# Reordered queues of the vector, scalar, GpSimd and DMA engines beside a fixed TensorE sequence

## The chip, the cores and the metric

The kernel runs on one core of one Trainium2 chip. The core has five engines with a queue of instructions each: TensorE (PE, with its weight loads PEld), VectorE (DVE), ScalarE (ACT), GpSimd (POOL) and SyncE (SP), which here issues DMAs. Each engine works through its own queue in order, and steps on different engines are tied together by semaphores. The metric is the time of one execution in microseconds; of several executions the median counts.

## The reference

The reference is a recurrent attention (RWKV-7) followed by a normalised SwiGLU feed-forward, all in float32. There are 4 x 8 heads, 768 steps of time, and head size 40. The state S of each head is a 40 x 40 matrix:

```
y[t]  = r[t] @ S
Sa    = S @ a[t]
S     = S * w[t] - outer(Sa, b[t]) + outer(v[t], k[t])
```

The outputs of all heads make up x with 3072 rows and 320 columns, and then

```
xn  = x / sqrt(mean(x*x) + 1e-6) * rms_g
g   = xn @ w_gate
out = (silu(g) * (xn @ w_val)) @ w_out        # w_gate, w_val: 320 x 1536
```

## The kernel before

The 768 steps of time are cut into 24 chunks of 32. The work falls into four kinds of stages, each of which puts its steps into a list (`Plan.add`, line 280):

- **front(c)** (line 652) loads r-independent inputs of chunk c on POOL's queue, turns them with TensorE, and builds products of decays by levels of 1, 2, 4, 8 and 16. It fills the triangular matrices LT by masked copies on VectorE (`where`, COPY_PREDICATED), among them three near the diagonal. After that LT goes to DRAM as sB in four quarters, and comes back in another layout as M in four parts, all on SP's queue.
- **inverse(c)** (line 760) solves a triangular system on VectorE: 31 pairs of `tmp` and `Yi` steps, each dependent on the one before. The result goes out as sY in parts and returns into LT in four quarters (LT<-sY). `early_inverse` (line 778) does this for the first four chunks in another way.
- **main(c)** (line 810) does the recurrence for chunk c: matmuls with the state and with LT, the copies of their results into VU, the new state ST, the scores As, and the output y by levels. It ends with the norm (x) and the scaled, turned xg. Two chunks make a group.
- **feed(g)** (line 939) does the feed-forward for a group of two chunks: 12 slices of weights, loaded again for each group into five buffers wf (wf<-sW, 480 KB each, on SP's queue). Each slice has matmuls into PSUM, a Silu on ScalarE (sg), a product on VectorE (hT), and matmuls into the accumulator po. `narrow` (line 973) makes the weights into float32 once, in the first third.

The order is written out by hand. `Plan.issue` (line 322) takes two long strings of numbers. ORDER has 6179 words. A word n stands for the n-th step from the first one that has not been issued yet, and "-" for a pair of filler matmuls that keep TensorE active. As the program is built in this order, each engine's queue is that order, cut down to its own steps. Moving a word so that it passes only words of other engines changes no queue.

PAIRS has one digit for each of 499 *rooms*. A room is the PSUM space of one result of TensorE, and the digit says which of three pairs of banks (the tiles ps) it gets. A room has its pair from the first matmul that writes it to the last step that reads it; the next room on the same pair has to wait for that. So a step of VectorE or ScalarE that reads a room is waited for twice: by those who use its result, and by TensorE when it wants the pair.

In the profile nearly all steps have the line of a helper: VectorE L444, ScalarE L464 (activation), L467 (copy) and L470 (scale), POOL L473, DMA issues L483, matmuls L486, and transposes on TensorE L489. Steps are told apart by their tiles and times.

The lines around which the masked copies and the inverse turn are these:

```
where(LT...[:, :, :, dist:], near[:, dist - 1:dist]..., g4[:, :, :, at:at + m])     # front, three times
tt(tmp, Y[:, 0:n, i:i + 1]..., M[:, i:i + 1, i + 1:]..., MUL)                       # inverse, 31 times
tt(Y[:, 0:n, i + 1:], Y[:, 0:n, i + 1:], tmp, SUB)
```

Of the kernel before, what the change touches and what calls it, by code (L numbers as in the profile page):

```python
# [102 lines left out]
0 181 565 549 548 544 599 344 566 345 15 564 551 237 0 345 346 551 395 560 347 544 561 397 348 0 236 558 3 544 348 545  # L103
237 554 573 349 561 350 586 351 397 570 572 352 0 553 396 565 394 551 4 567 397 552 438 395 570 349 581 350 571 572
562 351 5 352 353 354 355 398 563 578 579 0 563 398 665 399 355 356 0 356 572 357 4 399 524 0 357 522 358 7 359 573
577 512 360 574 513 8 572 361 581 362 363 582 364 365 580 401 366 9 583 10 411 405 406 0 409 405 403 0 403 425 392 393
0 390 575 396 572 355 408 356 574 357 358 407 359 573 718 360 361 400 434 362 717 363 435 364 398 365 707 368 0 402
705 366 403 365 708 404 718 408 405 707 0 0 713 576 0 576 577 578 406 383 407 441 0 407 571 408 383 2 409 0 577 571
409 578 2 579 718 580 0 47 218 219 220 293 48 221 356 49 222 0 222 357 610 223 356 369 775 49 620 279 361 776 374 50
619 362 293 51 280 609 52 373 66 372 282 360 385 383 55 224 628 225 226 56 295 627 227 618 386 2 418 228 384 294 3 617  # L110
71 1 382 398 229 395 394 0 0 172 348 173 174 349 175 300 176 0 13 176 177 1 178 300 179 180 181 182 309 183 304 308 2
311 3 0 180 317 308 301 318 220 316 13 181 315 0 298 217 299 219 178 308 218 19 220 179 6 229 326 180 309 330 325 181
324 0 229 181 182 183 328 184 309 322 185 220 186 0 186 187 231 188 0 270 188 189 317 271 190 234 280 237 0 215 277
329 330 331 315 224 328 13 314 0 414 222 226 339 225 20 229 0 230 339 183 227 321 184 185 223 186 232 322 233 187 331
188 189 330 190 4 191 234 192 332 323 235 333 193 231 195 5 194 6 241 236 0 236 542 237 544 241 336 535 335 239 545
334 0 332 0 236 530 193 408 531 240 532 241 409 242 541 7 243 411 244 245 548 246 338 339 0 336 243 190 337 547 735
338 546 193 339 545 4 244 191 608 744 551 13 245 552 745 192 246 563 0 729 545 0 542 556 747 17 553 567 241 737 558 2
543 242 736 570 566 746 552 582 568 551 569 547 579 578 591 555 590 334 3 554 8 335 563 565 564 0 561 8 335 336 547
337 548 0 335 336 546 6 337 555 338 339 14 340 0 340 6 397 341 571 342 343 0 548 391 337 562 393 338 563 0 548 393 434
564 391 558 568 338 435 339 567 340 341 394 342 560 343 573 0 574 343 573 394 661 395 0 343 557 344 0 567 394 518 344  # L120
345 509 346 347 397 508 569 348 349 573 519 3 350 400 351 398 8 401 568 352 578 353 354 576 355 0 352 573 5 353 354
575 395 398 402 438 355 400 404 6 356 357 403 401 358 0 358 576 404 398 359 577 405 360 578 406 361 575 407 652 408 0
361 362 410 363 364 411 409 365 0 718 365 407 366 369 710 388 368 411 707 367 412 709 651 413 389 719 414 653 415 717
580 416 581 720 582 725 583 417 584 708 585 586 663 587 726 981 588 370 418 589 727 0 586 415 736 1142 728 986 416 741
0 752 975 416 728 431 723 659 586 738 986 417 1142 572 441 418 751 749 739 421 587 573 748 588 366 589 761 750 426 0
589 367 725 783 0 589 982 590 367 762 591 658 981 365 420 592 991 2 593 659 992 771 758 722 594 0 594 424 595 420 596
429 597 722 598 599 0 0 8 3 309 308 311 178 179 224 180 9 181 182 10 304 225 183 184 227 185 0 182 183 317 301 343 184
0 178 179 6 295 0 300 295 15 310 179 216 304 16 308 214 307 225 326 305 321 180 322 181 0 319 225 181 182 324 333 305
# [5 lines left out]
398 546 542 13 547 401 231 550 3 574 232 543 560 233 544 0 230 231 541 581 545 554 555 550 438 553 330 331 332 232 333  # L134
552 0 333 564 570 571 567 232 566 565 550 579 561 0 0 332 395 333 576 560 575 0 333 573 560 395 396 435 662 570 397
521 334 335 512 336 337 400 572 338 522 339 340 511 341 0 570 404 579 402 581 405 400 578 5 580 401 0 405 0 339 408
405 340 406 341 342 407 401 582 343 344 583 4 345 409 581 346 347 580 348 410 349 411 415 350 351 5 352 353 416 6 412
0 347 708 348 349 350 710 0 350 351 716 434 352 353 405 708 354 406 435 355 409 706 356 0 356 717 357 409 358 718 410
359 411 716 360 648 361 412 0 361 412 362 0 412 362 576 721 365 577 413 578 363 579 580 647 364 581 722 987 582 583 0
583 975 735 648 584 722 585 976 413 723 383 727 414 586 441 0 727 984 657 738 383 2 739 586 737 3 414 571 587 751 1140  # L140
588 415 763 748 589 772 750 1 590 416 660 572 364 749 0 226 293 358 394 227 52 776 228 66 294 359 229 360 55 368 367
617 60 230 628 231 382 370 395 627 232 233 618 234 67 235 3 236 61 237 418 0 61 237 0 237 54 238 0 184 11 12 185 186
306 187 188 0 188 0 188 0 185 317 186 301 343 8 187 188 13 189 302 303 220 190 191 308 9 192 315 312 221 193 316 223
194 0 217 307 215 311 306 226 323 321 16 322 326 3 317 320 227 188 189 190 218 191 332 333 334 0 315 188 266 189 215
323 277 0 187 10 264 188 189 328 221 273 190 191 20 414 339 222 192 311 193 322 195 340 194 223 196 323 332 324 0 230
330 333 226 241 225 332 223 4 545 229 227 536 228 224 535 231 546 5 196 6 232 534 533 335 0 234 336 542 235 335 543
233 333 236 232 0 0 235 194 612 0 235 193 232 13 191 233 192 404 236 237 3 334 238 239 4 335 336 337 338 240 550 544
339 752 5 340 0 0 735 539 334 335 538 728 0 539 736 551 543 540 737 556 16 568 745 580 0 14 588 543 540 725 554 553
734 548 564 544 565 0 562 548 0 564 0 546 571 540 556 547 0 540 556 438 541 553 550 328 569 329 554 390 565 552 330 0
330 580 331 391 332 567 333 334 335 336 225 337 550 0 391 565 0 224 336 563 0 336 390 337 224 392 338 225 339 0 390  # L150
225 434 339 226 392 567 340 566 227 341 575 393 0 0 555 392 393 556 571 570 557 0 337 505 569 338 391 339 564 506 340
341 439 656 516 515 342 394 343 566 223 344 0 564 344 574 394 0 574 400 571 395 572 394 344 398 403 345 399 0 345 346
401 347 348 396 2 404 395 576 403 349 577 350 351 575 352 409 353 574 354 3 355 0 399 409 404 355 0 0 713 352 353 401
714 573 354 402 705 432 355 406 403 356 703 574 357 358 359 384 716 360 361 407 706 362 408 363 0 714 384 408 363 409
703 645 364 575 410 0 440 575 576 410 577 3 578 645 579 0 410 579 580 1 581 656 582 646 411 0 220 49 221 222 355 50
777 295 51 296 52 357 610 223 0 52 293 620 775 360 55 355 617 357 358 369 361 627 374 223 60 610 224 362 359 619 373
382 618 368 367 363 628 61 370 371 372 66 2 364 383 0 379 384 385 0 53 362 415 378 0 327 338 309 341 168 350 169 170
337 318 171 5 349 321 0 171 9 172 338 319 173 0 317 173 174 0 171 172 5 316 329 328 330 324 334 173 13 6 174 175 220
176 325 341 327 0 214 332 216 335 0 318 214 15 332 169 328 170 216 16 171 172 173 217 174 330 175 0 175 176 328 217
336 337 419 226 339 0 337 176 223 0 225 176 177 3 178 179 223 267 180 181 266 182 183 226 184 277 185 186 276 236 228  # L160
339 227 8 338 238 234 341 340 230 229 4 233 187 231 239 232 188 245 189 190 9 191 5 192 237 193 194 539 345 195 235
196 346 537 6 197 244 198 240 540 0 234 192 541 235 540 239 236 340 531 16 341 3 342 408 542 240 543 241 335 343 242
344 243 0 332 240 341 241 342 343 544 13 344 242 345 189 346 0 344 345 544 731 346 542 240 347 402 241 348 543 349 556
20 742 242 350 561 0 731 403 572 350 242 351 740 546 544 584 352 739 547 0 187 547 747 544 186 557 748 558 185 568 567
570 737 188 603 352 242 552 548 0 552 0 351 578 553 0 553 562 351 563 560 546 0 15 351 546 352 547 560 5 565 0 574 0
585 237 554 586 351 4 570 572 571 555 575 556 569 352 576 353 566 354 5 355 6 356 397 357 582 567 358 0 561 352 574
391 353 0 392 353 354 434 575 393 570 355 391 435 356 357 576 394 571 0 357 579 571 394 580 358 581 359 360 578 361
395 362 0 362 363 4 364 395 365 510 366 0 508 366 4 367 368 518 369 370 371 659 519 372 407 373 376 5 6 397 409 582 8
399 583 400 581 403 398 375 374 405 406 9 580 404 408 401 402 410 416 10 411 415 724 412 657 377 413 715 417 414 717 0
718 411 709 412 580 651 719 581 413 435 414 707 372 388 653 415 720 374 582 583 373 416 584 585 577 371 586 417 587  # L170
389 0 414 584 415 585 586 587 416 659 588 589 432 417 590 574 721 591 1143 592 593 1142 594 418 0 721 985 418 722 976
735 421 726 441 0 739 992 722 726 3 658 751 982 1 763 727 2 783 738 431 983 593 0 351 316 572 0 238 326 328 563 172
# [875 lines left out]
```

## Time and profile before

| what | value |
|---|---|
| three timed runs | 1074.34, 1081.09, 1081.99 us (median 1081.09) |
| the profiled execution | 1082.16 us, span of its instructions 1080.3 us |
| TensorE | 1023.1 us busy, 95% of the span |
| VectorE | 850.2 us, 79% |
| ScalarE | 470.6 us, 44% |
| POOL | 309.5 us, 29% |
| mean granted TensorE clock | 0.967 |

Busy time is the time in which an engine had an instruction at work. The page also follows back the chain of work that ended last, and says for each idle time what ended it. A row of a timeline has the start, the length, the engine, the line, the operation, what is written and read (out<-in), the shape and the count; in square brackets stand the idle time of the engine just ahead of it and what ended that. Rows with SPq are DMA issues in SP's queue: their length is that of the issue and not of the transfer. A row of stretches has the length, then busy time and count by engine, the granted clock, the DMA engines' share and GB/s.

### The profile page before, as it was taken

The page shows a single profiled execution, that of the slowest core. Times are in us where ns is not written, and L with a number is a line of the kernel's source. Part 1 is how long each engine was busy: PE and PEld are TensorE (multiplying, and loading weights), DVE is VectorE, ACT ScalarE, POOL GpSimd, SP SyncE. Part 2 cuts the span into 40 slices and gives each one's busy share as a digit, 9 for nine tenths or more (in the row PEclk, how much of TensorE's full clock was granted, in tenths as well). Part 3 has the DMA queues.
Part 4 walks back from the last instruction along what each step waited for, and adds up shares of the span by engine and source line. Part 5 has one row for each costly group of instructions (what it writes and reads, how often), then busy time and mean ns, then how long its engine had stood idle before and what let it go on. Part 6 is the DMA issues. An engine that isn't in the chain of part 4 may idle for free.

```text
span 1080.3 us, 53530 instructions
## 1 busy us (share of the span) xinstructions
PE 1023.1 (95%) x23406; PEld 840.3 (78%) x23406; DVE 850.2 (79%) x2861; ACT 470.6 (44%) x1043; POOL 309.5 (29%) x554
## 2 busy tenths in 40 slices
PE   6878899999999999999999999999999999999998
PEld 6767777877888777787778778778777887887876
DVE  7877768966868988888898789979879889797321
ACT  6846755743443434433434334434425334432211
POOL 9714504130532141341332231331322321210000
PEclk9677989999999999999999999999979999999999
DMA  9965428775564483664465555564636555444252
GB/s 179 206 149 121 73 67 217 227 151 158 126 153 122 105 170 90 152 124 129 123 148 119 129 144 113 126 137 131 153 71 145 123 129 144 121 116 113 79 151 75
DMA packets 172458, 143.35 MB, mean 133 GB/s; under 512 B 125504, under 2 KB 143872, under 8 KB 172224
## 3 DMA queue, kind: packets, MB, share of 16 engines
q1 hardware_dynamic: 153856, 116.96, 42.4%
q0 software_dynamic: 16192, 22.64, 11.9%
q8 instruction: 184, 3.01, 1.2%
q10 hardware_dynamic: 2176, 0.33, 0.3%
q14 instruction: 50, 0.41, 0.1%
HBM read 123.86 MB, written 15.99 MB: 129 GB/s over the span
## 4 chain that ended last, share of the span: by engine, by line
PE 73%; DVE 13%; DMA 5%; ACT 4%; issue 3%; SPq 1%; POOL 0%; ACTq 0%; DVEq 0%
PE ps L486 50%; PE po L486 12%; PE ps L489 9%; DVE LT L444 2%; DVE tmp L444 2%; DVE y L444 2%; DVE Yi L444 2%; SPq L483 1%; DVE K L444 1%; PE po L1015 1%; DMA LT<-sY 1%; DVE As L444 1%; DMA rn<-in_r_dram 1%; DMA wf<-in_moe_w_gate_dram 1%; DVE hT L444 1%
## 5 line engine op out<-in xcount | busy, mean ns | idle before, releaser
L486 PE MATMUL ps<-xg,wf 128*128 128x256 f32 (+1 forms) x1728 | 358.6, 395 | 4.2 <-DVE xg L444 1.9
L486 PEld LDWEIGHTS ps<-xg,wf 128*128 128x128 f32 (+1 forms) x1728 | 263.9, 191 | 61.6 <-issue 15.9
L486 PE MATMUL po<-wf,hT 128*128 128x320 f32 x576 | 179.9, 445 | 1.8 <-issue 1.3
L464 ACT ACTIVATE sg<-ps 128x256 f32<-128x256 f32 x144 | 53.5, 383 | 239.0 <-PE ps L486 236.4
L444 DVE TENSOR_TENSOR tmp<-Yi,M 128x60 f32<-128x60 f32 (+24 forms) x620 | 130.1, 210 | 17.1 <-DMA M<-sB 2.7
L444 DVE TENSOR_TENSOR Yi<-Yi,tmp 128x60 f32<-128x60 f32 (+24 forms) x620 | 129.8, 209 | 13.9
L483 POOL DMA_DIRECT2D VU<-in_v_dram x92 | 53.2, 584 | 285.9 <-PE ps L486 149.0
L486 PEld LDWEIGHTS po<-wf,hT 128*128 128x128 f32 x576 | 102.0, 189 | 37.3 <-issue 3.7
L444 DVE TENSOR_TENSOR hT<-ps,sg 128x256 f32<-128x256 f32 x144 | 59.5, 420 | 67.5 <-ACT sg L464 66.2
L444 DVE TENSOR_TENSOR K<-K,T 128x512 f32<-128x512 f32 (+1 forms) x192 | 93.9, 499 | 11.7 <-PE ps L486 5.4
L486 PEld LDWEIGHTS ps<-Ab,K 40*64 40x64 f32 x4608 | 78.9, 139 | 30.0 <-issue 10.5
L486 PE MATMUL ps<-Ab,K 40*64 40x56 f32 x4608 | 89.1, 226 | 11.2 <-issue 2.4
L467 ACT COPY K<-K 128x256 f32<-128x256 f32 (+1 forms) x168 | 71.3, 442 | 60.5 <-PE ps L486 42.8
L444 DVE TENSOR_TENSOR As<-ps,msi 128x256 f32<-128x256 f32 (+1 forms) x186 | 78.4, 475 | 15.8 <-PE ps L486 15.0
L467 ACT COPY KN<-ps 128x640 f32<-128x640 f32 x96 | 66.1, 690 | 54.2 <-PE ps L489 22.1
L483 POOL DMA_DIRECT2D kbn<-in_b_dram x92 | 53.5, 585 | 112.6 <-PE ps L486 112.0
L486 PEld LDWEIGHTS ps<-As,KN 128*40 128x40 f32 x3072 | 65.7, 124 | 14.9 <-issue 9.1
L486 PE MATMUL ps<-As,KN 128*40 128x32 f32 x3072 | 72.8, 204 | 1.5 <-issue 1.0
L483 POOL DMA_DIRECT2D kbn<-in_k_dram x92 | 53.5, 585 | 69.6 <-PE ps L486 69.6
L483 POOL DMA_DIRECT2D wn<-in_w_dram x92 | 51.3, 564 | 72.7 <-DVE KN L444 23.6
L444 DVE TENSOR_TENSOR y<-y,ps 128x256 f32<-128x256 f32 x119 | 49.9, 420 | 18.9 <-PE ps L486 16.3
L1015 PE MATMUL po<-ident 128*128 128x128 f32 x302 | 49.8, 319 | 6.6 <-DVE po L517 3.3
(133 smaller groups left out, 1560.4 us busy)
## 6 DMA issues: line engine op xcount, KB each, us to landing
wf<-sW SPq DMA_DIRECT2D x144, 480.0 KB, 4.2
M<-sB SPq DMA_DIRECT2D x80, 128.0 KB, 3.6
rn<-in_r_dram SPq DMA_DIRECT2D x24, 160.0 KB, 4.8
sW<-ex SPq DMA_DIRECT2D x16, 240.0 KB, 4.1
out_dram<-o SPq DMA_DIRECT2D x48, 80.0 KB, 4.2
kbn<-in_k_dram POOLq DMA_DIRECT2D x92, 40.0 KB, 3.8
kbn<-in_b_dram POOLq DMA_DIRECT2D x92, 40.0 KB, 3.6
wan<-in_a_dram POOLq DMA_DIRECT2D x46, 80.0 KB, 4.7
```

The lines of the kernel that those rows point to most:

```text
L444: plan.add("DVE", kind, lambda at: fn(at(o), *m(at)), [o], aps(*args))
L464: plan.add("ACT", "act", lambda at: nc.scalar.activation(at(o), at(a), f, **kw), [o] + aps(acc), [a])
L467: plan.add("ACT", "copy", lambda at: nc.scalar.copy(at(o), at(a)), [o], [a])
L483: plan.add(by, "dma", lambda at: queue.dma_start(out=o, in_=i), [o], [i])
L486: return o, lhsT, rhs, lambda at: nc.tensor.matmul(at(o), lhsT, rhs, start=start, stop=stop, skip_group_check=True)
L489: return o, i, ident, lambda at: nc.tensor.transpose(at(o), i, ident)
L1015: plan.warm = lambda: nc.tensor.matmul(po_[:, 0, DM:DM + P], ident, ident, start=False, stop=False, skip_group_check=True)
```

## The change

Only the two strings change. No step is added, removed or altered, and TensorE's sequence of matmuls and fillers stays the same, word for word. The first moved step belongs to front(9), at about 362 us of the profile, and the last ones to the weight loads of feed(10), at about 1000 us. At the least, these steps have been lifted out and put elsewhere in their queues:

| queue | steps | lifted | furthest, in places |
|---|---|---|---|
| VectorE | 2858 | 69 | 7 |
| ScalarE | 1024 | 9 | 4 |
| POOL | 545 | 13 | 4 |
| SP | 696 | 20 | 6 |

206 of the 499 rooms have another pair of banks. For most of these the three pairs have only changed names; 30 rooms follow another room on their pair.

Moves that the text speaks of, by the time of the step in the profile before:

- 365 us, VectorE: an inverse step goes from ahead of hT to five places later.
- 393 us, VectorE: a y step of main(7) goes ahead of four inverse steps, which come between the y steps.
- 533 us, VectorE: the third masked copy of front(13) goes behind a K multiply.
- 643 and 645 us, VectorE: an inverse step goes behind the small ss step of main(13), another behind its xg.
- 692 us, VectorE: xg of main(14) goes seven places ahead, in front of the second masked copy of front(17).
- 714 us, VectorE: hT of feed(6) goes ahead of a score step As and a y step.
- 740 us, VectorE: a VU copy of main(16) goes ahead of two inverse steps.
- 765 to 778 us, SP: one quarter of LT<-sY of inverse(17) goes behind its neighbour and three weight loads wf.
- 782 us, VectorE: a K multiply of front(19) goes behind the first masked copy, and an inverse step goes ahead of the third masked copy.
- 811 us, ScalarE: the scaling x of main(17) goes three places ahead.
- 828 us, SP: a weight load of feed(8) goes behind four sB transfers.
- 834 us, ScalarE: a K copy of front(20) goes four places back, behind two KN copies among others.
- 945 us, VectorE: an inverse step goes behind a VU copy of main(21).

The diff is of words in the strings. Its beginning shows how such moves look; for instance 549 548 544 599 344 566 has become 549 544 599 344 548 566, with the number behind a moved word changed where the count from the first open step has changed:

```
-0 181 565 549 548 544 599 344 566 345 15 564 551 237 0 345 346 551 395 560 347 544 561 397 348 0 236 558 3 544 348 545
-237 554 573 349 561 350 586 351 397 570 572 352 0 553 396 565 394 551 4 567 397 552 438 395 570 349 581 350 571 572
+0 181 565 549 544 599 344 548 566 345 15 564 551 237 0 345 346 551 395 560 347 544 561 397 0 236 3 544 237 545 558 347
+348 554 573 349 561 350 586 351 397 570 572 352 0 553 396 565 394 551 4 567 397 552 438 395 570 349 581 350 571 572
...
-1002212111100220021122202211200212210222111101220202000202212100002122212211000211100012222100000121211100002120120101
+1002212111100220012222202211200212120122111102001010110101121200110211121122000022200021111200000202012200001201201212
...
```

More of the change, by code (lines that the diff above doesn't have):

```diff
@@ L229 @@
 0120112210001221122012220021200102101012220201011212001111212202210111000021002021211120221110102222111211210012011000
-1002212111100220021122202211200212210222111101220202000202212100002122212211000211100012222100000121211100002120120101
-1022002210210202000100110200101221011111200122222002221212222111212222110000102202200100221011020200110202212210011112
-1121002022200122222010011000101100002122220122200211111100221212110210011222201102110022000221102222221111100020002111
+1002212111100220012222202211200212120122111102001010110101121200110211121122000022200021111200000202012200001201201212
+2111110021012020222121221011221001211122011100000210002020000222100000221111210010011211002100212100220202220002222211
+2121002011100122222010012111011100000122021022212000000011220200112010000222211120112200022001122222221111100020202111
 021101012121211211120120120
```

176 rows, old and new, of the table ORDER are left out of this document.

## The prediction, made before the result was known

> **What bounds the kernel now.** I read three views: the page's busy shares and 40 slices, then busy time by stretches, then TensorE's waits. The page first:
>
> ```profile
> span 1080.3 us, 53530 instructions
> PE 1023.1 (95%) x23406; PEld 840.3 (78%) x23406; DVE 850.2 (79%) x2861; ACT 470.6 (44%) x1043; POOL 309.5 (29%) x554
> PEclk9677989999999999999999999999979999999999
> PE 73%; DVE 13%; DMA 5%; ACT 4%; issue 3%; SPq 1%; POOL 0%; ACTq 0%; DVEq 0%
> ```
>
> TensorE carries the kernel: 95% busy, and 73% of the chain that ended last. The clock line shows one dip far from the start, a 7 in slice 30. The stretches (columns: length, then busy time of PE, PEld, DVE, ACT and POOL with counts, clock, DMA share, GB/s) show the part that the change touches:
>
> ```profile
> 340.00:1000.00 660.00, 642.84 (x15084) 523.72 (x15084) 566.24 (x1963) 262.34 (x591) 181.85 (x311) 0.99 0.54 128
> 784.26:787.67 3.41, 2.02 (x132) 1.82 (x133) 3.26 (x10) 1.41 (x4) 0.00 (x0) 1.00 0.45 149
> 787.67:801.33 13.66, 13.66 (x230) 11.00 (x232) 8.55 (x26) 3.60 (x7) 2.31 (x4) 0.50 0.24 46
> 801.33:804.74 3.41, 3.41 (x211) 3.37 (x208) 2.04 (x6) 0.05 (x1) 1.65 (x3) 1.00 0.50 121
> 716.00:719.41 3.41, 2.12 (x49) 1.41 (x53) 2.81 (x10) 0.00 (x0) 3.26 (x6) 1.00 0.43 74
> ```
>
> From 340 to 1000 us TensorE idles 660.00 - 642.84 = 17.16 us. Its order is kept, so this is all that a better order of the others can give directly. Part of it hangs on no neighbour's order, as two rows of TensorE's waits say:
>
> ```profile
> PE ps L486 <- issue: 3.3, 8, 0.8
> PE po L486 <- issue: 1.3, 1, 1.3
> ```
>
> 4.6 us of "issue" stays. At most 17.16 - 4.6 = 12.6 us is left, in some thirty waits, mostly for VectorE.
>
> There is a second way to gain or lose. From 787.67 to 801.33 us the clock was 0.50 and TensorE was busy all the while: 13.66 x 0.5 = 6.83 us lost, one time only in this part. Just before, in 3.41 us, TensorE had been busy 2.02 us (59%). A stretch of the same length with 2.12 us (62%) at 716 us kept the full clock. So the clock here falls somewhere between 1.29 and 1.39 us of idle time in 3.41 us. The three timed runs (1081.09, 1081.99, 1074.34) differ by 6.75 to 7.65 us, about one such stretch: I read the fast one as a run without it.
>
> **The change part by part.** All instructions stay, and with them every duration. The price of each move is the wait it lengthens or shortens. I went through the moved steps one by one, each against TensorE's wait nearest behind it.
>
> *Chain steps ahead of filler on VectorE.* Most moves put a step of an inverse (tmp and Yi, wanted only tens of microseconds later) behind a step that TensorE waits for. Two clear sites:
>
> ```profile
> 532.74 0.73 DVE L444 COPY_PREDICATED LT<-near,ps 128x128 f32<-128x128 uint32 x1
> 533.09 0.63 DVE L444 TENSOR_TENSOR K<-K,T 128x256 f32<-128x256 f32 x1
> 533.87 0.35 PE L486 MATMUL ps<-Ab,K 40*64 40x56 f32 x9 [0.47 <-DVE K L444]
> 739.36 0.24 DVE L444 TENSOR_TENSOR tmp<-Yi,M 128x75 f32<-128x75 f32 x1
> 739.63 0.24 DVE L444 TENSOR_TENSOR Yi<-Yi,tmp 128x75 f32<-128x75 f32 x1
> 739.90 0.48 DVE L444 COPY VU<-ps 32x320 f32<-32x320 f32 x1
> 740.53 0.73 PE L489 MATMUL ps<-ident,VU 128*104 128x128 f32 x5 [0.47 <-DVE tmp L444]
> ```
>
> At 533 us the K multiply goes ahead of the last masked LT copy: it starts at 532.74 instead of 533.09, so 0.35 us of the 0.47 us wait goes. What comes late next is LT, which TensorE does not need there. At 740 us the VU copy passes two inverse steps, 739.90 - 739.36 = 0.54 us: all of the 0.47 us wait goes. Together **0.82 us**.
>
> *The same with less in it.* Each row below is a wait of TensorE whose releaser moves forward, the last one by ScalarE:
>
> ```profile
> 365.98 0.44 PE L489 MATMUL ps<-ident,x 128*128 128x128 f32 x2 [0.68 <-DVE hT L444]
> 395.35 0.33 PE L489 MATMUL ps<-ident,y 128*128 128x128 f32 x1 [0.16 <-DVE y L444]
> 646.14 0.70 PE L486 MATMUL ps<-xg,wf 64*128 64x256 f32 x4 [1.00 <-DVE xg L444]
> 692.94 0.49 PE L486 MATMUL ps<-xg,wf 64*128 64x256 f32 x2 [0.28 <-DVE LT L444]
> 945.53 0.28 PE L486 MATMUL ps<-VU,KN 64*40 64x40 f32 x7 [0.27 <-DVE Yi L444]
> 811.43 0.40 PE L489 MATMUL ps<-ident,K 104*128 104x104 f32 x2 [0.25 <-ACT Sd L467]
> 834.37 0.40 ACT L467 COPY K<-K 128x256 f32<-128x256 f32 x1
> 834.67 0.68 ACT L467 COPY KN<-ps 128x640 f32<-128x640 f32 x1
> 835.41 0.81 PE L486 MATMUL ps<-Ab,K 40*64 40x56 f32 x40 [0.83 <-ACT KN L467]
> ```
>
> One inverse step of about 0.2 us is passed at 365.98, 646.14 (two of them, one early in its chain) and 945.53; where independent steps overlap by 0.1 us that is worth 0.13, 0.25 and 0.2. At 395.35 the y chain is interleaved with inverse steps, which closes gaps: 0.16. At 692.94 and 811.43 the wait is for a PSUM pair; a step ready long before (xg, x) now frees a pair earlier, and the new pairs hand that one over: 0.28 and 0.25. At 835 us the KN copy goes before a K copy: 834.67 - 834.37 = 0.30. Sum **1.57 us**. About ten more moves of this kind touch waits of 0.1 to 0.4 us; I give them 0.6 us together, between 0 and 2.
>
> *The stretch before the slow clock.*
>
> ```profile
> 781.43 0.79 PE L486 MATMUL ps<-Xs,LT 32*32 32x40 f32 x64
> 782.15 1.07 PE L486 MATMUL po<-wf,hT 128*128 128x320 f32 x3
> 782.31 0.42 DVE L444 TENSOR_TENSOR K<-K,T 128x256 f32<-128x256 f32 x1
> 782.64 2.23 DVE L444 COPY_PREDICATED LT<-near,ps 128x384 f32<-128x384 uint32 x3
> 784.93 1.16 PE L486 MATMUL ps<-Ab,K 40*64 40x56 f32 x64 [1.44 <-DVE LT L444]
> 787.63 0.67 PE L486 MATMUL ps<-Ab,K 40*64 40x56 f32 x14 [0.53 <-ACT KN L467]
> 764.07 0.94 SPq L483 DMA_DIRECT2D LT<-sY  x2
> 777.64 0.32 SPq L483 DMA_DIRECT2D wf<-sW  x1
> wf<-sW SPq DMA_DIRECT2D x144, 480.0 KB, 4.2
> LT<-sY SPq DMA_DIRECT2D x80, 32.0 KB, 3.6
> ```
>
> The K multiply goes between the LT copies and an inverse step behind it, filling gaps between dependent copies: about **0.2 us**. Against it stands the one large lengthening. One of four LT transfers, issued as the second of this row of two from 764.07, goes behind three weight loads, and two of those wait on TensorE; the last was issued at 777.64. The LT transfer now starts at 777.64 + 0.32 = 777.96 and with 3.6 us lands at 781.6, later if the 480 KB in front hold it up (the page's 4.2 us for a weight load gives 781.84 for that, plus the LT itself). The matmuls that read it started at 781.43. Behind them stand one out group and then the 1.44 us wait for the LT copies. So up to about 1.2 us of lateness comes out of that wait and costs nothing; only a landing after 782.8 costs. I take 0, between 0 and 0.5.
>
> *Queue order of DMAs elsewhere.* The other moved weight loads, sB, M and sY quarters, and input loads on POOL trade places with neighbours, mostly of their own group. The longest way is that of a weight load that goes behind four sB transfers:
>
> ```profile
> 828.16 0.32 SPq L483 DMA_DIRECT2D wf<-sW  x1
> 853.59 0.70 PE L486 MATMUL ps<-xg,wf 64*128 64x256 f32 x4
> ```
>
> It was issued 25.4 us before its first reader; 12 us later it still lands in time at 4.2 us. I take 0 for all of these, between 0 and 0.5. A step that a reordered step now stands behind may wait longer; the sites above are those where TensorE stands next in line.
>
> **Sum:** 0.82 + 1.57 + 0.6 + 0.2 = 3.2 us of waits, ends 0 and 6. The profiled execution took 1082.16 us (span 1080.3), 1.07 above the median of the timed runs, 1081.09. 1082.16 - 3.2 = 1079.0 for a like profile; against the median, 1077.9. **Forecast 1078.**
>
> One rule speaks against counting on the clock. The Trainium skill, "TensorE: Matmul & The Clock Gate", section "HAM oscillation — how this bites in real kernels", asks only for no idle gaps over about 3.4 us. By that rule gaps of 1.44 and 0.53 us could not have cost the clock, and trimming them could not restore it: 1078 and no other mode. The rows at 784.26 and 787.67 disagree: 1.39 us idle went ahead of the fall.
>
> **The rivals.** *A: the slow stretch goes.* The LT lateness takes idle time from 784 to 781.4 us, and the cluster's idle time, 1.44 + 0.53 and small ones, spreads over 6 us instead of 4; if no 3.41 us then holds more than about 1.3, the clock stays: 1077.9 - 6.8 = 1071.1. For it: the trims point the right way, and one run of before seems to have had it. Against: the boundary lies within 0.1 us of my estimate, and where the stretches of 3.41 us begin need not be the same in each run. *B: the trims do not reach the end.* TensorE arrives earlier and waits at the next site (VectorE was busy 566.24 of 660 us, 86%): 1081. *C: slower.* A second slow stretch, at 718 us: TensorE idles 1.29 us there already, for "issue"; 0.1 us more within the same 3.41 us decides, and work that now arrives some us earlier can fall so. Price 6.83: 1077.9 + 6.8 = 1084.7.
>
> **How the numbers follow.** Forecast 0.50, A 0.28, B 0.11, C 0.09, 0.02 beyond. Within 1% means 1070.3 to 1091.9; 1% is about what a measurement of this kernel tells from no change, as the three runs spread over 0.7%. Faster by over 1% takes the lower part of A: 0.12. Slower takes what lies beyond C: 0.04. The rest, 0.84, is within. The range runs from the middle of A, lowered by the unknown trims, to C: 1069.5 to 1085.
>
> **What would show it.** Right: the waits at 533, 740, 693 and 835 us gone or under half; TensorE's idle time from 340 to 1000 us near 14 us. For A: clock 1.00 throughout from 150 us on. For C: 0.50 after 718 us. Wrong: a wait for the LT transfer at 781 us of over 1.5 us, or the sum of waits unchanged with "issue" grown.

## The result, and the profile after

The changed kernel took 1072.86 us (median of 20 runs, 1066.39 to 1084.23); the kernel before, run beside it, 1080.29 us (median of 20). The ratio is 0.9936, 95% interval 0.9917 to 0.9955: about 6.9 us faster, between 4.9 and 9.0. The forecast was 1078, range 1069.5 to 1085: direction and range held, but the 3 us forecast were less than half of what came.

The page of the changed kernel: span, busy shares, granted clock in 40 slices, the chain that ended last.

```profile
span 1072.0 us, 53523 instructions
PE 1013.8 (95%) x23406; PEld 834.0 (78%) x23406; DVE 847.4 (79%) x2861; ACT 469.9 (44%) x1043; POOL 310.2 (29%) x554
PEclk9876999999999999999999999999999999999999
PE 73%; DVE 12%; DMA 4%; ACT 4%; issue 4%; SPq 2%; POOL 0%; ACTq 0%; DVEq 0%; POOLq 0%
```

TensorE bounds the kernel as before. The dip of the clock line in slice 30 is gone. The stretches say the same (length, then busy time of PE, PEld, DVE, ACT and POOL with counts, clock, DMA share, GB/s):

```profile
340.00:1000.00 660.00, 643.45 (x15362) 525.62 (x15361) 565.15 (x1970) 264.76 (x597) 181.12 (x310) 1.00 0.54 129
777.34:780.76 3.42, 2.48 (x89) 1.71 (x88) 3.32 (x9) 1.55 (x4) 0.00 (x0) 1.00 0.39 150
780.76:784.17 3.41, 2.87 (x190) 2.58 (x181) 3.32 (x10) 1.60 (x4) 0.00 (x0) 1.00 0.46 149
784.17:787.58 3.41, 2.80 (x83) 2.44 (x80) 3.03 (x11) 2.29 (x5) 1.17 (x3) 1.00 0.12 23
```

TensorE's matmuls are the same 23406 in the same order in both profiles, so they can be laid side by side by number. Up to the matmul at 340 us of before, the changed kernel is 0.8 us ahead, over code that is the same in both. Then it gains 3.3 us up to the one at 780 us, 0.4 us more up to 787.7, 4.7 us in the stretch that had run at half clock (787.7 to 801.4 us of before), and loses 0.5 us net from there to 1060 us. So in this pair of executions over half of the gain is the clock. (The stretches of half clock in the traces are 3.41 us or whole multiples of it long, but for the one that the end of the program cuts; the text counts stretches of 3.41 us from their edges.) Whether that is the change or luck could not be read from two profiles.

TensorE's waits from 340 to 1000 us, first the remaining row of "issue" of the kernel before, then the changed kernel (what it waited for, us in total, times, longest):

```profile
PE ps L489 <- issue: 0.2, 1, 0.2
```

```profile
PE ps L486 <- issue: 6.8, 11, 0.9
PE ps L486 <- ACT KN L467: 1.3, 3, 0.7
PE ps L486 <- DVE xg L444: 1.2, 2, 0.9
PE ps L486 <- DVE LT L444: 1.2, 3, 0.6
PE ps L486 <- DMA LT<-sY: 0.9, 1, 0.9
...
PE po L486 <- issue: 0.3, 1, 0.3
```

"issue" grew from 3.3 + 1.3 + 0.2 = 4.8 to 7.1 us. All other idle time fell from 17.16 - 4.8 = 12.4 to 660.00 - 643.45 - 7.1 = 9.45 us, by 2.9 us. The forecast had 3.2 us for it. Two waits of the changed kernel, though, are longer than they were, ahead of the matmuls that started at 738.90 us without a wait and at 749.02 us behind one of 0.04 us in the kernel before:

```profile
735.31 1.16 PE L486 MATMUL ps<-Ab,K 40*64 40x56 f32 x64 [0.28 <-DVE Yi L444]
745.28 1.15 PE L486 MATMUL ps<-Ab,K 40*64 40x56 f32 x64 [0.41 <-DVE LT L444]
```

The forecast named no such price. Around the LT transfer the chain went as the prediction had it (TensorE's timeline of the changed kernel, and SP's queue):

```profile
777.31 0.27 PE L486 MATMUL ps<-Xs,LT 32*32 32x40 f32 x6
778.52 0.76 PE L486 MATMUL ps<-Xs,LT 32*32 32x40 f32 x58 [0.94 <-DMA LT<-sY]
779.21 1.34 PE L486 MATMUL po<-wf,hT 128*128 128x320 f32 x4
780.48 1.16 PE L486 MATMUL ps<-Ab,K 40*64 40x56 f32 x64
773.89 0.43 SPq L483 DMA_DIRECT2D LT<-sY  x1
```

TensorE now waits 0.94 us for the late transfer, and the 1.44 us wait for the LT copies behind it is gone. Together with the 0.19 and 0.53 us behind it (now 0 and 0.40), the waits of this site came down from 2.16 to 1.34 us: 0.82 us less, where 0.2 had been forecast.

### The profile page after: what moved, and what is told of

It is laid out like the page before. It is cut to its first block, busy times and chain, and to the rows that moved or that the text cites. A ratio compares the mean times of both kernels' runs of the same rounds, so it can differ in the third digit from the quotient of the medians.

```text
span 1072.0 us, 53523 instructions
## 1 busy us (share of the span) xinstructions
PE 1013.8 (95%) x23406; PEld 834.0 (78%) x23406; DVE 847.4 (79%) x2861; ACT 469.9 (44%) x1043; POOL 310.2 (29%) x554
## 3 DMA queue, kind: packets, MB, share of 16 engines
q8 instruction: 184, 3.01, 1.2%
## 4 chain that ended last, share of the span: by engine, by line
PE 73%; DVE 12%; DMA 4%; ACT 4%; issue 4%; SPq 2%; POOL 0%; ACTq 0%; DVEq 0%; POOLq 0%
PE ps L486 50%; PE po L486 13%; PE ps L489 9%; SPq L483 2%; DVE As L444 2%; DVE tmp L444 1%; DVE y L444 1%; DVE Yi L444 1%; DVE K L444 1%; ACT ex L464 1%; DVE LT L444 1%; DMA wf<-in_moe_w_gate_dram 1%; DMA wf<-in_moe_w_val_dram 1%; DVE hT L444 1%; DVE wf L444 1%
## 5 line engine op out<-in xcount | busy, mean ns | idle before, releaser
L486 PE MATMUL ps<-xg,wf 128*128 128x256 f32 (+1 forms) x1728 | 353.1, 391 | 3.7 <-DVE xg L444 1.9
L486 PEld LDWEIGHTS ps<-xg,wf 128*128 128x128 f32 (+1 forms) x1728 | 260.8, 188 | 59.3 <-issue 16.5
L486 PEld LDWEIGHTS ps<-Ab,K 40*64 40x64 f32 x4608 | 76.6, 136 | 30.9 <-issue 11.0
L486 PE MATMUL ps<-Ab,K 40*64 40x56 f32 x4608 | 86.6, 222 | 12.6 <-issue 4.2
```

Of the source, the lines that this page charges most:

```text
L486: return o, lhsT, rhs, lambda at: nc.tensor.matmul(at(o), lhsT, rhs, start=start, stop=stop, skip_group_check=True)
```

## The experiments

Two theories stood against each other. **Theory 1:** the moves near 784 us keep the clock up, and most of the gain hangs on them. **Theory 2:** the many small trims carry it, and the half clock is chance. The 84 places at which the queues differ lie apart from each other, so that each can be changed alone; TensorE's sequence is the same in all kernels but those with fillers.

### Only the five places near 784 us

```
 order of before, and in it, between 763 and 785 us:
+ one LT<-sY transfer behind three wf loads (SP)
+ K multiply between the masked LT copies; three inverse steps moved (VectorE)
```

> The kernel before, with only the moves issued between 763 and 785 us (five places of 84: the LT transfer behind three weight loads, the K multiply between the masked LT copies, three inverse steps). Theory 1, the clock: these moves spread TensorE's idle time so that no 3.41 us hold more than about 1.3 us of it; the stretch of half clock after 784 us goes, TensorE's clock is 1.00 from 340 to 1000 us. In the two profiles the same matmuls took 4.7 us less over that stretch, so 4.7 to 5.5 us less than before, ratio 0.995. Theory 2, the trimmed waits: the gain lies in the many small waits elsewhere and the half clock comes and goes by chance: at most 0.7 us less, ratio 0.999 to 1.000.

Measured: 1076.38 us (12 runs), ratio 0.9993, interval 0.9967 to 1.0019. The profile had the clock at 1.00 over the whole part, as theory 1 said; the time was as theory 2 said.

### All but these five

```
 order of after, and in it, between 763 and 785 us:
- the five places (put back to the order of before)
```

> The changed kernel with the five places between 763 and 785 us put back to the old order; the other 79 stay. Theory 1, the clock: TensorE again idles 1.4 us for the LT copies, the stretch of half clock is back in the profile (13.7 us at 0.50), and of the gain some 2.2 to 3.3 us are left: ratio 0.997 to 0.998. Theory 2, the trimmed waits: nearly the whole gain stays, 6 to 7 us: ratio 0.994.

Measured: 1073.49 us, ratio 0.9943, interval 0.9913 to 0.9973. Theory 1 fell as the main account: with the old order near 784 us nearly the whole gain stays (5.5 of 6.2 us by the means over all runs; the five places alone gave 1.0). The half clock did not come back there in the profile, although the wait of 1.44 us did.

### The late LT transfer alone

```
 order of before, and in it, one place:
-LT<-sY wf wf wf
+wf wf wf LT<-sY
```

> The kernel before, with one place of the 84 changed: the quarter LT transfer goes behind the three weight loads, nothing else. Theory 1 in its sharp form, lateness alone: TensorE waits 0.8 to 1.2 us for the transfer, the wait for the LT copies falls from 1.44 us to 0.3 to 0.6 us, the idle time falls into two windows of 3.41 us and the clock stays at 1.00: 4 to 5 us less, ratio 0.995 to 0.996. Rival: the lateness is neutral and it is the K multiply among the LT copies that ends the 1.44 us wait; then the half clock stays and the ratio is 0.999 to 1.001.

Measured: 1076.87 us, ratio 0.9978, interval 0.9955 to 1.0000. TensorE's timeline of this kernel:

```profile
780.97 0.76 PE L486 MATMUL ps<-Xs,LT 32*32 32x40 f32 x58 [1.04 <-DMA LT<-sY]
781.65 1.34 PE L486 MATMUL po<-wf,hT 128*128 128x320 f32 x4
783.17 1.16 PE L486 MATMUL ps<-Ab,K 40*64 40x56 f32 x64 [0.18 <-DVE LT L444]
```

The lateness is 1.04 us, and the wait behind it falls from 1.44 to 0.18 us, with the K multiply where it was. That part is shown. The gain of 4 to 5 us is not: the interval ends at 4.9 us and at 0.

### The kernel before once more

> The kernel before, unchanged, a second profile. Theory 1 in its strong form, the old order always loses the clock after 784 us: 13.7 us at 0.50 there again. Theory 3, chance: the wait of 1.44 us for the LT copies is there again, with 0.19 and 0.53 us behind it, but whether the clock falls depends on where the 3.41 us windows begin; with all but the five places the clock stayed in a window that was busy 0.58, so I expect it to stay here, 1.00 from 760 to 810 us, at 60 to 40.

One profile, with no edit. The half clock was there again, 13.65 us long; my 60 to 40 was on the wrong side. Its stretches, and then those of the kernel with only the early places (below), which has the old order near 784 us too:

```profile
782.44:785.86 3.42, 1.98 (x128) 1.76 (x128) 3.27 (x10) 0.97 (x3) 0.00 (x0) 1.00 0.43 144
785.86:799.51 13.65, 13.26 (x216) 10.60 (x216) 8.93 (x27) 3.70 (x7) 2.32 (x4) 0.50 0.24 44
```

```profile
783.59:787.01 3.42, 1.98 (x68) 1.38 (x66) 3.28 (x7) 0.63 (x2) 0.00 (x0) 1.00 0.48 149
787.01:801.00 13.99, 12.28 (x512) 10.58 (x504) 12.42 (x38) 5.01 (x10) 4.04 (x8) 1.00 0.34 71
```

TensorE was busy 1.98 of 3.42 us in both; behind the one the clock fell, behind the other it stayed. The waits are the same in both (1.44, 0.19 and 0.53 us); only where the stretches of 3.41 us begin differs. In the two profiles of the kernel before they begin 0.67 and 1.12 us ahead of the end of the 1.44 us wait, and hold the matmuls of the small shapes behind it; in the other 2.39 us ahead, with a large out group ahead of the wait in it. Of seven profiles with the old order here two lost the clock (both of the kernel before), five did not; with the new order none of three did. In three of the five the stretches cut the cluster of waits in two, so that none was busy less than 2.2 us.

The same matmuls tell what the half clock costs here. From 787.7 to 801.4 us of the kernel before they took 5.2 us less in each of the five profiles that kept the clock. That is less than the 6.83 us of clock that the stretch loses: at full clock TensorE runs into waits of 0.58 and 0.21 us there, at matmuls 17757 and 17829, which neither profile at half clock shows.

### Early and late places

```
 order of before, and in it:
+ the 56 places before 763 us     (first kernel)
+ the 23 places after 785 us      (second kernel)
```

> The kernel before, with only the 56 places that are issued before 763 us changed. In the profiles the same matmuls from 340 to 780 us took 3.3 us less in the changed kernel and 1.8 us less with all but the five places near 784 us; theory 1, trimmed waits early: 2 to 3.5 us less than before, ratio 0.997 to 0.998, and over half of what the 79 places gave (5.6 us). Rival, the late moves carry it: at most 1 us less, ratio 0.999 to 1.000.

> The kernel before, with only the 23 places that are issued after 785 us changed. The profiles show no gain between 801 and 1060 us (the changed kernel loses 0.5 us there, the one with all but five places is even): theory 1: within 1 us of before, ratio 0.999 to 1.001. Rival, the late moves carry the rest of the 5.6 us: 2 to 3 us less, ratio 0.997 to 0.998.

Measured: early 1073.96 us, ratio 0.9975, interval 0.9945 to 1.0005; late 1076.98 us, 0.9995, interval 0.9959 to 1.0031. Both lie where theory 1 of these expectations, trimmed waits early, had them. The early interval reaches past 1, so the time alone does not show it.

### Engines and queues

```
 order of before, and in it, of the 56 early places:
+ the 45 where only VectorE or ScalarE steps move   (first kernel)
+ the 11 where SP's or POOL's steps move            (second kernel)
```

> The kernel before, with those 45 of the early 56 places changed where only VectorE and ScalarE steps move, and the PSUM pairs that go with them; the queues of SP and POOL as before. Taken over all runs so far, the time at equal clock stands 4.4 us below before with the early places, 4.8 us with all but the five near 784 us. Theory, trimmed waits on VectorE and ScalarE: 3 to 4.4 us of that are here, ratio 0.996 to 0.9975. Rival, the order of the DMA queues (a transfer that no longer stands in the way of another): at most 1 us here, ratio 0.999 to 1.000.

> The kernel before, with the other 11 of the early 56 places: those where steps of SP's and POOL's queues move (in one place VectorE steps beside them). Theory, trimmed waits on VectorE and ScalarE: within 1 us of before, ratio 0.999 to 1.001. Rival, the order of the DMA queues: 3 to 4.4 us less, ratio 0.996 to 0.9975.

Measured: 1078.13 us, ratio 0.9984 (0.9953 to 1.0015), and 1076.88 us, ratio 0.9986 (0.9960 to 1.0012). Each lies between its two expectations, and both intervals hold 1: by time this is undecided. The waits tell more. The table lays the profiles side by side by matmul number: TensorE's idle time in us just ahead of the matmul that starts at the given time of before.

```
                    366.0  395.4  490.7  533.9  613.5  646.1  692.9  738.9  740.5  749.0  784.9  811.4  945.5
before               0.68   0.16   0.68   0.47   0.47   1.00   0.28   0.00   0.47   0.04   1.44   0.25   0.27
before, once more    0.68   0.17   0.67   0.47   0.47   1.00   0.24   0.00   0.47   0.04   1.44   0.25   0.27
LT transfer alone    0.68   0.17   0.00   0.48   0.48   0.70   0.27   0.00   0.45   0.04   0.18   0.24   0.27
only the five        0.69   0.17   0.22   0.47   0.48   1.00   0.26   0.00   0.47   0.04   0.04   0.24   0.27
late places          0.68   0.17   0.00   0.48   0.48   1.00   0.25   0.00   0.45   0.04   1.44   0.00   0.00
early, queues        0.69   0.17   0.00   0.47   0.48   0.85   0.27   0.00   0.47   0.04   1.45   0.25   0.27
early, engines       0.42   0.00   0.00   0.00   0.18   0.88   0.00   0.27   0.00   0.41   1.44   0.25   0.27
early places         0.40   0.00   0.00   0.00   0.17   0.87   0.00   0.29   0.00   0.41   1.44   0.25   0.26
all but five         0.40   0.00   0.00   0.00   0.17   0.87   0.00   0.29   0.00   0.41   1.44   0.00   0.00
after                0.40   0.00   0.00   0.00   0.17   0.88   0.00   0.28   0.00   0.41   0.00   0.00   0.00
```

Most of these waits repeat to 0.04 us from run to run, and each goes exactly in the kernels that hold its own place, the early ones with the VectorE and ScalarE moves (365.98 to 740.53 us), the late ones with the late moves. The new waits at 738.9 and 749.0 us come with the same VectorE and ScalarE moves. Two columns are no evidence: 490.73 us, a wait for an LT transfer, comes and goes by itself, and 646.14 us went to 0.70 and 0.85 us in kernels without its move.

### What the timed runs say at equal clock

Timed runs come with their mean granted clock, but for the twenty of the kernel before that stand beside the changed kernel; for that kernel the runs of the later sessions are used. A straight line through 219 of them (each kernel with a constant of its own; the kernel with 45 more fillers, below, left out) gives 0.55 us of time for each us of (1 - clock) x time, with 2.8 us of scatter. By it the difference to before splits (the +- are 95%):

```
                    mean time   at equal clock   by the clock
after                 -6.2        -4.1 +- 1.4     -2.1 +- 1.0
all but five          -5.5        -5.1 +- 1.7     -0.4 +- 1.6
early places          -4.7        -4.4 +- 1.7     -0.3 +- 1.2
early, engines        -1.4        -3.1 +- 1.7     +1.7 +- 1.2
early, queues         -2.5        -1.3 +- 1.8     -1.2 +- 1.5
late places           -0.4        -0.4 +- 1.7      0.0 +- 1.9
only the five         -1.0        -0.3 +- 1.7     -0.7 +- 1.3
LT transfer alone     -2.1        -0.5 +- 1.7     -1.5 +- 1.2
```

The three kernels with the new LT transfer (43 runs) have a mean clock of 0.9789, the six with the old one (152 runs) 0.9764: 0.0025 +- 0.0012 apart if every run counts by itself, or 2.7 us of 1078. That is 0.4 of a stretch of 13.65 us at half clock, which fits a stretch that comes in some four of ten executions with the old order, as in two of the seven profiles. But kernels of one order differ by as much: 0.9784 with the early queue moves and 0.9735 with the early engine moves, both with the old transfer, against 0.9775 with only the five places and the new one. This is a fit and a count, not a run in which the stretch was switched on and off, and the clock's part of the gain is argued and not shown.

### Fillers in the waits

If idle time costs the clock, filler matmuls in a wait should win it back.

```
 order of before, ahead of the matmuls that wait 1.44 us for LT:
+- - - - - -
```

> The kernel before with no move at all, but six filler steps (12 matmuls of 0.11 us, 1.34 us) ahead of the matmuls that wait 1.44 us for the LT copies; this adds work and shortens no wait of another engine. Theory 1, the clock: TensorE is busy through the gap, the clock stays at 1.00 and the kernel is 4 to 6 us faster, ratio 0.995. Theory 2: fillers in a gap change nothing: ratio 1.000 (0.999 to 1.001).

> The six filler steps again, a second profile; its timed runs were 6.7 us slower than before at a lower mean clock (0.971 against 0.976), but the profiled one was the fastest of them. Theory A: the filler's 24 instructions shift what comes after them against the places, 127 matmuls apart, where TensorE stops for issue, and a stretch of half clock appears after 784 us (7 to 14 us at 0.50). Theory B: the lower clock lies in the first 340 us and is chance: clock there 0.91 or less, and 1.00 after 340 us.

Measured: 1085.73 us, ratio 1.0065, interval 1.0034 to 1.0095, slower. By the line above, 3.8 of the 7.1 us of mean difference stand at equal clock and 3.3 go by the clock. In the first profile, a run of 1079.07 us, the clock held after 784 us, as theory 1 had it. The second profile, a run of 1095.4 us and so longer than all twelve timed ones (1079.07 to 1093.27):

```profile
787.01 1.50 PE L1015 MATMUL po<-ident 128*128 128x128 f32 x12
788.63 1.16 PE L486 MATMUL ps<-Ab,K 40*64 40x56 f32 x64
789.97 0.82 PE L486 MATMUL ps<-VU,KN 64*40 64x40 f32 x64 [0.19 <-DVE tmp L444]
791.32 1.14 PE L486 MATMUL ps<-Ab,K 40*64 40x56 f32 x61 [0.53 <-ACT KN L467]
793.67 0.32 PE L486 MATMUL ps<-Ab,K 40*64 40x56 f32 x3 [1.21 <-issue]
...
795.59 1.56 PE L486 MATMUL ps<-Ab,K 40*64 40x56 f32 x64 [0.58 <-DVE LT L444]
792.73:796.14 3.41, 1.88 (x47) 1.57 (x51) 2.02 (x6) 2.06 (x4) 0.83 (x2) 1.00 0.02 5
796.14:806.38 10.24, 10.24 (x176) 8.06 (x168) 5.31 (x18) 1.30 (x3) 1.48 (x3) 0.50 0.41 85
```

The fillers fill the gap. But an "issue" wait of 1.21 us now stands in the middle of a group, between its 61st and 62nd matmul, and the clock falls right behind it, and once more at 840 us. The stop is at matmul 17758 of TensorE's sequence, in the other profile of this kernel too (0.91 us). In the kernels without fillers 17757 is the first matmul of a group that waits 0.58 us for LT, so that a stop there is hidden by that wait. The fillers pushed the work by 12 matmuls against the stop, and the wait for LT still comes, 0.58 us, behind it. How often the clock falls at this stop, two profiles do not tell. The sum of the "issue" waits was no higher than usual in them, 20.7 and 17.8 us over the whole span, where the ten profiles with the old count had 14.3 to 20.1.

The stops have fixed places. Over 340 us they stand, in all profiles of the kernels with the old count, at the matmuls 10004, 10132, 11021, 16235, 18648, 18776 and 19922 (or the next), multiples of about 127 apart, of different length in each run and sometimes absent. The page has a pair of queues that fits (queue, kind: packets, MB, share of 16 engines):

```profile
q8 instruction: 184, 3.01, 1.2%
q14 instruction: 50, 0.41, 0.1%
```

3.42 MB over 53523 instructions are 64 bytes each, and 3.01 MB in 184 packets 256 instructions each, or 128 matmuls with their weight loads. So I read the stops as instructions that arrive late. That reading is argued from the spacing; no run separates it.

### Fillers in the first 140 us

To look for a kernel that beats both:

```
 order of after, ahead of the waits at 45.8, 63.5, 73.5, 85.4 and 136.8 us:
+14, 14, 9, 2 and 6 fillers          (first kernel)
+ only the 6 at 136.8 us             (second kernel)
```

> The changed kernel with 45 more filler steps (0.223 us each) in five waits of the first 140 us that stand ahead of half clock in its profile (3.33, 3.47, 2.25, 0.68 and 1.59 us), each within the wait's length. If only the clock counted: the stretches of half clock from 47 to 84 us and at 136 us go (3.4 + 6.8 + 10.2 us at 0.50, some 10 us lost in all), of which 0.6 reaches the end: 5 to 7 us less than the changed kernel, about 1067 us, ratio to before 0.988. Rival: the 180 added instructions shift all that follows against the places, 127 matmuls apart, where TensorE stops for issue, as the six fillers near 784 us did (ratio 1.0065): no gain or a loss, 1073 to 1080 us.

> The changed kernel with six more filler steps (12 matmuls, 1.34 us) in one of the five places of the filler run before, the wait of 1.59 us at 137 us. Theory, the work against the issue stops: nothing is lost in the wait itself, but all that follows is shifted by 12 matmuls against the places, 127 apart, where TensorE stops for issue; the sum of issue waits rises above the 12 to 19 us of the profiles with the old count, to 22 us or more, and the kernel is 4 us or more slower than the changed one, 1077 us or more. Rival, the other four filler places made the loss of 3.5% (they delayed the start of something): here the clock stays at 1.00 at 137 us and the time is 1070 to 1073 us, ratio to before 0.991 to 0.994.

Measured: 1116.5 us, ratio 1.0346 (1.0297 to 1.0394), and 1087.16 us, ratio 1.0072 (1.0042 to 1.0102). TensorE's waits for "issue" over the whole span: of the changed kernel, of the second filler kernel, of the first one (its code stands one line lower):

```profile
PE ps L486 <- issue: 17.4, 26, 1.6
PE po L1015 <- issue: 2.4, 1, 2.4
PE po L486 <- issue: 0.3, 1, 0.3
```

```profile
PE ps L486 <- issue: 17.7, 22, 2.0
PE ps L489 <- issue: 3.8, 4, 2.5
PE po L1015 <- issue: 3.6, 3, 2.1
PE po L486 <- issue: 2.3, 2, 1.5
```

```profile
PE ps L487 <- issue: 44.6, 38, 2.8
PE po L1016 <- issue: 2.4, 1, 2.4
```

20.1 us with the old count, 27.4 with six fillers more, 47.0 with 45 more. The clock of the second kernel stayed at 1.00 at 137 us, but that shows nothing: it was 1.00 there in the changed kernel's profile too, which has no half clock at 136 us, though the first expectation says so. It fell elsewhere, at 156, 214, 795 and 839 us. At 795 us it did so behind the same stop as with the fillers near 784 us, which now stands behind the 62nd matmul of the group:

```profile
791.94 1.15 PE L486 MATMUL ps<-Ab,K 40*64 40x56 f32 x62 [0.81 <-ACT KN L467]
794.32 0.32 PE L486 MATMUL ps<-Ab,K 40*64 40x56 f32 x2 [1.23 <-issue]
```

The loss was 14 us against the changed kernel, where 4 or more had been expected. In neither kernel did the fillers delay the work at their own places: by 140 us the first was 0.3 us and the second 1.2 us ahead of the changed kernel. The loss came behind them, 31 and 9 us by the matmul at 780 us of the changed kernel, 46 and 16 by that at 1000 us. No better kernel came of it.

## Why the prediction was right or wrong

**The sum of waits** was 3.2 us, and the waits other than "issue" fell by 2.9 us in the profile; the timed runs were 4.1 +- 1.4 us shorter at equal clock. The mechanism held, and the size came out, in part by luck: the 2.9 us have in them the 0.68 us at 490.73 that come and go, and, the other way, waits of 0.61, 0.21 and 0.18 us at matmuls 17757, 17829 and 17965 that stand in all profiles with the old count but the two that lost the clock there. By site: 533 and 740 us 0.47 each (0.82 forecast for both, 0.94 came), 395 us 0.16, 692 us 0.28 and 811 us 0.25 as forecast, 945 us 0.27 for 0.2, 366 us 0.28 for 0.13. Too high were 646 us (at most 0.12 for 0.25) and 835 us: 0.30 forecast, 0.10 in the profile, where the wait went from 0.83 to 0.73 us. That wait is 0.03 us in the second profile of before, so there was nothing firm to trim. Among the unnamed sites, 613 us gave 0.30. What the sum put at nothing is the delay of steps that now come behind moved ones: with the VectorE and ScalarE moves came 0.28 us of new wait at 738.9 and 0.37 at 749.0, more than the VU copy won at 740 us. The site near 784 us, with 0.82 us for the 0.2 forecast, makes up for it.

**The LT lateness at no cost** held: 0.73 to 1.04 us of new wait in the three kernels that have it, against the 1.2 allowed, and 1.26 to 1.44 us less behind it.

**TensorE's idle time near 14 us** did not come, 16.55 did: "issue", which I had put down as constant at 4.6, was 7.1. It varies by itself, from 4.8 to 8.4 us in the ten profiles with the old count.

**What failed is the step on the clock.** It had three parts. The boundary, "somewhere between 1.29 and 1.39 us of idle time in 3.41 us", is no boundary: 1.44 us of idle in 3.42 kept the clock in one profile and lost it in another. A's price, 6.83 us, was too high: the stretch at half clock costs 5.2 us there. And A was set up as a rival that happens or does not, in the median. The stretch came in two profiles of seven with the old order, and the timed runs split into 4.1 +- 1.4 us at equal clock and 2.1 +- 1.0 us by the clock. So the result, 1072.86, lies between the forecast and A, nearer to A, and the likely account is that both work at once: trims, and a stretch that comes less often. That the 2.1 us are this stretch is not shown; they hold every stretch of the run. The sign set for A, clock 1.00 from 150 us on, was there in the profile of the changed kernel up to 1070 us, but in those of the late places and the early queues, with the old order near 784 us, as well: one profile cannot tell. Reading the fast run of the three, 1074.34, as a run without the stretch was unfounded as well: the runs of before spread over 1069 to 1092 us (one of 3777 us left aside), with the half clock of the first 140 us and the length of the stops different in each profile.

The rule of the Trainium skill that I had weighed ("TensorE: Matmul & The Clock Gate", section "HAM oscillation — how this bites in real kernels": no idle gaps over about 3.4 us) is too weak here: twice the clock fell with no gap above 1.44 us ahead of it. The same page of the Trainium skill says in its part on the clock gate ("What's actually happening") that the window is free-running and does not reset when a kernel starts; the profiles with the same three waits and different fates agree with that.

**B**, trims that do not reach the end, is refuted as a whole for the early places by the split at equal clock (4.4 +- 1.7 us), though the waits at 738.9 and 749.0 us are a piece of it; for the late places it stays possible (0.4 +- 1.7 us). **C** did not occur in any profile: the clock held at 718 us, where the stop was 0.32 to 1.33 us long.

## What to carry to other kernels

Compare profiles of one instruction order matmul by matmul: waits between engines repeat to a few hundredths of a us and can be trimmed and counted one by one, while clock dips and "issue" waits vary from run to run and must be judged over many runs. Keep the bounding engine's sequence as it is when trimming: 24 instructions added in an idle gap cost 7 us here, though they fitted the gap. Look also for the step that each moved one pushes back. A price that depends on chance enters the forecast with its share, not as all or nothing.

## What the runs showed of the hardware

TensorE stopped for "issue" at fixed matmul numbers, about 127 or multiples of it apart, for up to 2.8 us. 12 matmuls of filler at 137 us brought the sum of these stops from 20.1 to 27.4 us, 12 near 784 us left it at 20.7 and 17.8; in three profiles of these kernels one stop, at matmul 17758 or 17759, fell into the middle of a group, with 0.91, 1.21 and 1.23 us, and behind the two longer ones the clock fell. The granted clock can fall after 3.41 us in which TensorE was busy 58 to 59% and no gap exceeded 1.44 us, and can stay at the same share. The two stretches of the kernel before that lost it held only matmuls of small shapes behind the wait; two other stretches speak against this as the rule. With the LT transfer alone the clock fell at 158.06 us behind 3.41 us that were busy 1.86 us with large matmuls only (11 of 64x256 and 128x256); with the early places it stayed at 165.77 us behind 3.41 us that were busy 1.87 us with small ones but for one. What decides stays open, and no run set the phase of the stretches.
